# Running sums of a Strassen-like last layer: one three-bank tile against three one-bank tiles

## Chip, cores and metric

The kernel runs on one core of one Trainium2 chip. The metric is the device time of the whole program in microseconds (us). Beside it the profile gives the span: from the first to the last instruction of one profiled execution.

## What is computed

The reference is cut to what matters. All matrices are fp32 in and out.

```python
def _attn_ref(q, k, v, p):                       # q, k, v: 4 x 8 x 576 x 64; p: 4 x 8 x 32 x 64
    p_packed = sm_attn(p, k, v)
    return sm_attn(q, p_packed, p_packed)

def _moe_ref(x, domain_probs, w1, w2):           # x: 2304 x 512, four experts
    p = domain_probs / (domain_probs.sum(-1, keepdims=True) + 1e-09)
    for e in range(E):
        out += p[:, e:e + 1] * (np.maximum(x @ w1[e], 0.0) @ w2[e])

def _moe2_ref(x, w_in, w_out, s, b):             # 512 -> 2048 -> 512
    r = np.maximum(x @ w_in, 0.0)
    g = s * (r * r) + b
    return g @ w_out
```

The change lies in the last function: in `g @ w_out`, and in the order of the steps that make `g`.

## The kernel before

**Stages.** Attention and the four experts fill the first part of the program; the last layer begins to run beside them and has TensorE for itself from about 700 us on. An fp32 product is made of three fp32r matmuls: high part by low part, high by high, low by high.

**The last layer.** The 2048 hidden columns are cut into 4 groups `g` of 512, the 2304 tokens into 3 pairs `tp` of 384-token tiles. One (g, tp) is called a round here; there are 12. In a round both products go by Strassen's scheme (in Winograd's form): seven block products `k`, named "11", "12", "s2", "s1", "s3", "s4", "22" in place of eight. `m3` (matmuls on L1052, 384 columns) is the first product, `x @ w_in`: 7 products times 2 column blocks `j`, which makes 14 units of six matmuls each. Its sums leave PSUM by ACT and DVE (L1109, L1111, L1117, L1118) into `z`.

**The gate.** `z` becomes `g` in place: `q_relu` (L1127, ACT), `q_gate` with n = 0 a square (L1132, ACT) and n = 1 scale and bias (L1134, ACT), for each of four quarters "11", "12", "21", "22" (`f"{c + 1}{j + 1}"`). `q_sum` (L1146, DVE) forms the four Strassen sums of the quarters. `q_part` splits each of the seven operands into the high part (n = 0, L1155, ACT) and the low part (n = 1, L1158, DVE); these are the tiles `gg`.

**The second product.** In the rounds with g = 0 it is `m4` (L1168): plain, 512 columns, 12 matmuls to each of six 128-token blocks; a finished block is copied to `o_sb` by ACT (L1176). In the rounds with g > 0 it is `m4_next` (L1184): for each product `op` in the order `LAST` = "12", "11", "s2", "s1", "s3", "s4", "22" and each 128-token block i = 0, 1, 2 six matmuls of 256 columns. A product adds to a running sum in PSUM: "12", "s1" and "s4" to the right half of a bank (`cols`, h = 1), "11", "s2", "s3" and "22" to the left half (h = 0), bank i for block i. After each product the half is added to `o_sb` by DVE (L1196): all three blocks with one 128x768 instruction, and in the very last round one block at a time, 128x256. The three banks are one tile, `o_ps`. Finished rows go to `out` by SP's queue (L1200).

**The order of the work.** All engines run their own queue in program order, and the program is written by hand. A unit i of the last loop first issues what the table `weave` holds for this step (`at(step, fn, ...)`, L1511 to L1526 for the gate), then the six `m3` matmuls, then a share of the waiting list `todo` (9 matmuls of `m4_next`, about 5 of `m4`). The second product of a round goes on the list four units after its round has ended. So in PE's queue units of 6 + 9 matmuls alternate. After the last unit of `m3` only the list is left: the tail.

**PSUM.** Of 8 banks `o_ps` takes three; five more, "b0" to "b4" of `take_b`, hold `m3`'s sums in turn.

Of the kernel before, what the change touches and what calls it, by code (L numbers as in the profile page):

```python
# [8 lines left out]
F32 = mybir.dt.float32  # L9
# [10 lines left out]
def attention_experts_mlp_kernel(  # L20
# [42 lines left out]
    T3 = 384  # L63
    NT3 = NT // T3
    NS = T3 // P
# [626 lines left out]
    HK = KB // 2  # L692
# [251 lines left out]

    def take_b(name):
        tag = free_b.pop(0)
        return tag, ps_o.tile([P, DM], F32, tag=tag, name=name)

    def x_flip(i, n):
        tag, t = take_b(f"xf_{n}")  # L950
# [6 lines left out]
        )  # L957


    xs, gg, o_sb, sx, yy, o_ps = {}, {}, {}, {}, {}, []  # L960
    xs_dram = {
        (tp, k): dram.tile([P, 2, HK, T3], F32, name=f"xs_dram{tp}{k}")
        for tp in range(NT3 // 2) for k in range(len(OPS))
# [197 lines left out]
    NTP = NT3 // 2  # L1161

    def m4(g, tp, i, f, n):
        acc = o_ps[0][:, i % 3, :]
        y = gg[g, tp, f // 2, i // NS][:, :, f % 2, (i % NS) * P : (i % NS + 1) * P]
        wh, wl = wo_t[g * FG + f]
        lhsT, w = ((y[:, 0], wl), (y[:, 0], wh), (y[:, 1], wh))[n]
        nc.tensor.matmul(  # L1168
            acc, lhsT=lhsT, rhs=w,
            start=(f == 0 and n == 0), stop=(f == FG - 1 and n == 2),  # L1170
        )
        if f == FG - 1 and n == 2:
            t, i = 2 * tp + i // NS, i % NS
            if i == 0:
                o_sb[t] = keep.tile([P, NS, DM], F32, tag="x2", bufs=XB, name=f"o_sb{t}")
            nc.scalar.activation(o_sb[t][:, i, :], acc, AF.Copy)  # L1176

    def m4_next(g, tp, k, i, n):
        op = LAST[k]
        h = int(op in ("12", "s1", "s4"))  # L1180
        cols = slice(h * HK * P, (h + 1) * HK * P)
        r, m = divmod(n, 3)
        x, w = ((0, 1), (0, 0), (1, 0))[m]
        nc.tensor.matmul(  # L1184
            o_ps[0][:, i, cols],
            lhsT=gg[g, tp, k][:, x, r, i * P : (i + 1) * P], rhs=wov[g, k][:, w, r, :],
            start=(n == 0 and op in ("11", "12")), stop=(n == 5), skip_group_check=True,
        )
        end = (g, tp) == (NG - 1, NTP - 1)
        if n == 5 and (end or i == NS - 1):  # L1190
            b = slice(i, i + 1) if end else slice(0, NS)
            c, d = {"11": (0, 0), "12": (0, 0), "s2": (0, 1), "s1": (1, 1), "s3": (1, 1),
                    "s4": (0, 1), "22": (1, 0)}[op]
            t = 2 * tp + c
            dst = o_sb[t][:, b, d * HK * P : (d + 1) * HK * P]
            nc.vector.tensor_tensor(out=dst, in0=o_ps[0][:, b, cols], in1=dst, op=ALU.add)  # L1196
            if g == NG - 1 and op in ("s4", "22"):
                for j in range(b.start, b.stop):
                    r0 = t * T3 + j * P
                    nc.sync.dma_start(out=out[r0 : r0 + P], in_=o_sb[t][:, j])  # L1200


    with tc.manual_schedule():
# [136 lines left out]
        def at(step, fn, *args):  # L1340
            weave.setdefault(step, []).append((fn, args))
# [153 lines left out]
        for g in range(1, NG):  # L1495
            u0 = pos((g * NTP - 1) * UP)
            for q in range(g * NQ, (g + 1) * NQ):
                at(u0 - 5, load_wi, q)
            at(u0 - 2, wi_sums, g, 0)
            for k in range(NK):  # L1500
                at(u0 + 2 * k + 1, wop_parts, g, k)
                if k == 1:
                    at(u0 + 3, wi_sums, g, 1)
                for tp in range(NTP):
                    at(pos((g * NTP + tp) * UP + 2 * k) - 9, xs_load, g, tp, k)
            at(u0 + UP + 1, load_wov, g)
            at(u0 + UP + 4, wov_sums, g, 0)
            at(u0 + UP + 9, wov_sums, g, 1)
            for k in range(NK):
                at(u0 + UP + 6 + 2 * k + 6 * (g == 1 and k > 3), wov_parts, g, k)  # L1510
            for tp in range(NTP):  # L1511
                i = pos((g * NTP + tp) * UP)
                for j in range(NQ):
                    for d, n in ((3, 0), (9, 3), (11, 1)):
                        at(i + d + j, q_relu, g, tp, j, n)
                    for c in range(2):
                        for n in range(2):
                            at(i + 12 + c + j + n, q_gate, g, tp, f"{c + 1}{j + 1}", n)
                for n in range(2):
                    at(i + 14 + n, q_part, g, tp, 1, n)  # L1520
                    at(i + 15 + n, q_part, g, tp, 0, n)
                for d, what in ((16, "s1"), (16, "s2"), (18, "s3"), (19, "s4")):
                    at(i + d, q_sum, g, tp, what)
                for k in range(2, NK):
                    for n in range(2):
                        at(i + 13 + 2 * k + n, q_part, g, tp, k, n)  # L1526
# [34 lines left out]
        stack_a.close()  # L1561
        gb = ctx.enter_context(tc.tile_pool(name="gb", bufs=1, reuse_waits="tile"))
        gate_pool.append(gb)
        ps_o = ctx.enter_context(tc.tile_pool(name="ps_o", bufs=1, space=PSUM, reuse_waits="tile"))
        o_ps.append(ps_o.tile([P, NS, DM], F32, name="o_ps"))
        todo = []
        due = 0.0

# [68 lines left out]
```

## Time and profile before

| | |
|---|---|
| device time, median of 3 runs | 1130.6 us (1122.51 to 1138.27) |
| the profiled execution, its own device time | 1124.23 us |
| its span | 1122.4 us |
| mean granted TensorE clock, share of full speed | 0.996 |
| PE busy | 1065.6 us (95%) |
| DVE busy | 683.6 us (61%) |
| ACT busy | 538.0 us (48%) |

PE is TensorE's matmuls, PEld its weight loads, DVE VectorE, ACT ScalarE, POOL GpSimd, SP the engine that issues the DMAs. A matmul's row begins when it starts and ends when its result is written; matmuls overlap in the array, so a busy PE can still be late. In the views a time in square brackets is how long the engine stood idle before the row, and behind the arrow what released it. A granted clock of 1.00 is 2.4 GHz.

### The profile page before, as it was taken

The numbers are of one execution on the slowest core, as the hardware profiler recorded it, in microseconds if no ns is written. First come the engines' busy times: TensorE is split into PE (matmuls) and PEld (weight loads), VectorE is DVE, ScalarE is ACT, GpSimd is POOL, SyncE is SP. The second block draws the span as 40 slices with busy tenths as digits, with TensorE's granted clock in tenths as the row PEclk, the third lists the DMA queues.
The fourth block names the chain that finished last, engine by engine and source line by source line (L and its number), as shares of the span: only waits on it lengthen the run. The fifth ranks groups of instructions, "written<-read, shape, count | busy, mean of one in ns | idle before, by whom it ended". The sixth has DMA issues, their size and how long they took to land.

```text
span 1122.4 us, 18145 instructions
## 1 busy us (share of the span) xinstructions
PE 1065.6 (95%) x6701; PEld 923.5 (82%) x6701; DVE 683.6 (61%) x1293; ACT 538.0 (48%) x1165; POOL 211.2 (19%) x222
## 2 busy tenths in 40 slices
PE   8999999999999999999999999989898999999975
PEld 5878788888888888888888888877798888888964
DVE  7886755564562455653656457874257676776663
ACT  3533334543442433433357567545555665656650
POOL 1521130321000310103212220120221141141000
PEclk9999999999999999999999999999999999999999
DMA  9765025957865556758552333546454545454411
GB/s 263 186 126 95 3 86 190 307 170 197 256 238 136 145 146 207 236 187 217 150 160 90 108 131 132 225 183 229 166 199 146 188 168 205 169 187 165 164 58 56
DMA packets 106899, 187.09 MB, mean 167 GB/s; under 512 B 49449, under 2 KB 63785, under 8 KB 106811
## 3 DMA queue, kind: packets, MB, share of 16 engines
q1 hardware_dynamic: 106539, 185.87, 52.9%
q8 instruction: 53, 0.87, 0.3%
q14 instruction: 35, 0.29, 0.1%
q10 hardware_dynamic: 272, 0.07, 0.0%
HBM read 131.11 MB, written 54.79 MB: 166 GB/s over the span
## 4 chain that ended last, share of the span: by engine, by line
PE 83%; ACT 8%; DVE 5%; DMA 2%; issue 1%; SPq 0%; ACTq 0%; DVEq 0%
PE acc L889 35%; PE h L843 18%; PE h L1052 11%; PE o_ps L1184 10%; PE o_ps L1168 3%; DVE o_sb L1196 2%; PE pp L625 2%; ACT z L1134 2%; ACT z L1132 1%; DVE qs L1146 1%; DMA v<-in_v_dram 1%; ACT gg L1155 1%; DVE gg L1158 1%; PE pw L539 1%; ACT gg L1023 1%
## 5 line engine op out<-in xcount | busy, mean ns | idle before, releaser
L843 PEld LDWEIGHTS h<-a,w1p 128*128 128x128 f32 x1536 | 229.1, 188 | 27.0 <-issue 5.6
L843 PE MATMUL h<-a,w1p 128*128 128x320 f32 (+1 forms) x1536 | 248.3, 297 | 1.0 <-DVE hl L866 1.0
L866 DVE SCALAR_TENSOR_TENSOR hl<-h,hh 128x256 fp32r<-128x256 f32 x256 | 107.6, 420 | 218.3 <-ACT rest L864 111.6
L1052 PE MATMUL h<-xs,wop 128*128 128x384 f32 x1008 | 205.1, 339 | 1.3 <-DVE xt L910 1.3
L864 ACT ACTIVATE hh<-h 128x256 fp32r<-128x256 f32 x256 | 98.6, 385 | 223.3 <-PE h L843 220.1
L889 PE MATMUL acc<-w2l,hh 128*128 128x512 f32 x512 | 201.7, 394 | 0.0
L889 PE MATMUL acc<-w2h,hh 128*128 128x512 f32 x512 | 201.3, 393 | 0.0
L889 PE MATMUL acc<-w2h,hl 128*128 128x512 f32 x512 | 200.4, 391 | 0.0
L1184 PE MATMUL o_ps<-wov,gg 128*128 128x256 f32 x1134 | 163.2, 288 | 32.9 <-DVE o_sb L1196 22.6
L1184 PEld LDWEIGHTS o_ps<-wov,gg 128*128 128x128 f32 x1134 | 147.0, 190 | 53.1 <-DVE o_sb L1196 16.2
L1052 PEld LDWEIGHTS h<-xs,wop 128*128 128x128 f32 x1008 | 174.5, 190 | 6.3 <-DVE xt L910 1.6
L889 PEld LDWEIGHTS acc<-w2h,hl 128*128 128x128 f32 x512 | 96.2, 188 | 21.9
L889 PEld LDWEIGHTS acc<-w2l,hh 128*128 128x128 f32 x512 | 96.4, 188 | 15.0 <-DVE xt L914 0.3
L889 PEld LDWEIGHTS acc<-w2h,hh 128*128 128x128 f32 x512 | 96.3, 188 | 13.2
L1196 DVE TENSOR_TENSOR o_sb<-o_ps,o_sb 128x768 f32<-128x768 f32 (+1 forms) x77 | 62.4, 810 | 48.3 <-PE o_ps L1184 47.9
L1168 PE MATMUL o_ps<-wo,gg 128*128 128x512 f32 x216 | 61.0, 404 | 12.8 <-ACT o_sb L1176 12.8
L1158 DVE TENSOR_TENSOR gg<-z,gg 128x768 fp32r<-128x768 f32 x45 | 45.2, 1004 | 28.4 <-ACT gg L1155 28.2
L1168 PEld LDWEIGHTS o_ps<-wo,gg 128*128 128x128 f32 x216 | 40.0, 190 | 23.2 <-ACT o_sb L1176 18.0
L688 POOL TENSOR_TENSOR w2l<-w2r,w2h 128x512 fp32r<-128x512 f32 x24 | 31.7, 1329 | 107.7 <-ACT w2h L685 107.6
L1127 ACT ACTIVATE z<-z 128x384 f32<-128x384 f32 x54 | 27.8, 519 | 42.0 <-DVE z L1118 41.8
L633 DVE TENSOR_TENSOR w1o<-pp,w1o 128x512 fp32r<-128x512 f32 x48 | 29.8, 683 | 20.8 <-ACT w1o L632 20.8
L941 ACT ACTIVATE x<-xt 32x384 f32<-32x384 f32 x80 | 41.7, 522 | 1.3
(449 smaller groups left out, 1337.2 us busy)
## 6 DMA issues: line engine op xcount, KB each, us to landing
xs<-xs_dram SPq DMA_DIRECT2D x63, 768.0 KB, 4.2
w1p_dram<-w1o SPq DMA_DIRECT2D x48, 512.0 KB, 4.1
w1p<-w1p_dram SPq DMA_DIRECT2D x192, 128.0 KB, 4.2
xs_dram<-xs SPq DMA_DIRECT2D x21, 768.0 KB, 3.3
w1r<-in_moe_w_dram SPq DMA_DIRECT2D x12, 512.0 KB, 4.4
w2r<-in_moe_w_dram SPq DMA_DIRECT2D x24, 256.0 KB, 5.4
out_dram<-o_sb SPq DMA_DIRECT2D x18, 256.0 KB, 2.1
v<-in_v_dram SPq DMA_DIRECT2D x8, 512.0 KB, 9.6
```

The costliest lines, as they stand in the source:

```text
L633: nc.vector.tensor_tensor(out=t[:, 1], in0=ps[x, z], in1=f32(t[:, 0]), op=ALU.subtract)
L688: nc.gpsimd.tensor_tensor(out=lo, in0=raw_t.pop((e, f)), in1=f32(hi), op=ALU.subtract)
L843: nc.tensor.matmul(t[:, : width(bi, hf)], lhsT=w1p_block(e, bi, f, gi, w), rhs=a2[bi][:, x, gi, part(bi, hf)], start=(n == 0), stop=(n == ...
L864: nc.scalar.activation(hi, src, AF.Relu)
L866: nc.vector.scalar_tensor_tensor(out=lo, in0=src, scalar=0.0, in1=f32(hi), op0=ALU.max, op1=ALU.subtract)
L889: nc.tensor.matmul(acc[j], lhsT=x, rhs=w, start=(f == 0 and n == 0), stop=(g == NF - 1 and n == 2),)
L941: nc.scalar.activation(dst[32 * q : 32 * q + 32, a], src[:, q], AF.Copy)
L1052: nc.tensor.matmul(ps, lhsT=w[:, a, col], rhs=x[:, z, m, :], start=(fresh and n == 0), stop=(n == 3 * HK - 1), skip_group_check=chain,)
L1158: nc.vector.tensor_tensor(out=t[:, 1], in0=src, in1=f32(t[:, 0]), op=ALU.subtract)
L1168: nc.tensor.matmul(acc, lhsT=lhsT, rhs=w, start=(f == 0 and n == 0), stop=(f == FG - 1 and n == 2),)
L1184: nc.tensor.matmul(o_ps[0][:, i, cols], lhsT=gg[g, tp, k][:, x, r, i * P : (i + 1) * P], rhs=wov[g, k][:, w, r, :], start=(n == 0 and op i ...
L1196: nc.vector.tensor_tensor(out=dst, in0=o_ps[0][:, b, cols], in1=dst, op=ALU.add)
```

## The change

Four things change. First, `o_ps` becomes three tiles of one bank each, "o0", "o1", "o2"; in `m4` block i takes tile i % 3, allocated anew for each block. Second, `m4_next` deals the pairs of product and block over the banks in another way: block 1 lies in bank 1 (left or right half as before), blocks 0 and 2 lie side by side in bank 0 for "11", "s2", "s3", "22" and in bank 2 for "12", "s1", "s4". DVE adds block 1 with one 128x256 instruction when it is done, and blocks 0 and 2 with one 128x512 instruction when block 2 is done, in all rounds, the last one included. Third, the pools are split so that "b0" to "b2" take the first three banks, the running sums the next three, "b3" and "b4" the last two. Fourth, in the gate's order the quarters "11" and "12" come one step earlier, and the high and low parts of "12" and "11" come at steps 13 and 14 where they came at 15 and 16 ("12") and at 14 and 15 ("11").

```diff
     def take_b(name):
         tag = free_b.pop(0)
-        return tag, ps_o.tile([P, DM], F32, tag=tag, name=name)
+        pool = ps_x if tag in ("b0", "b1", "b2") else ps_z
+        return tag, pool.tile([P, DM], F32, tag=tag, name=name)
...
     def m4(g, tp, i, f, n):
-        acc = o_ps[0][:, i % 3, :]
+        if f == 0 and n == 0:
+            o_ps[i % 3] = ps_o.tile([P, DM], F32, tag=f"o{i % 3}", name=f"o_{g}{tp}{i}")
+        acc = o_ps[i % 3]
...
     def m4_next(g, tp, k, i, n):
         op = LAST[k]
-        h = int(op in ("12", "s1", "s4"))
-        cols = slice(h * HK * P, (h + 1) * HK * P)
+        b = int(op in ("12", "s1", "s4"))
+        bank = 1 if i == 1 else 2 * b
+        half = b if i == 1 else i // 2
+        if (bank, "next") not in o_ps:
+            o_ps[bank, "next"] = ps_o.tile([P, DM], F32, tag=f"o{bank}", name=f"on_{bank}")
+        ps = o_ps[bank, "next"].rearrange("a (h c) -> a h c", h=2)
...
         nc.tensor.matmul(
-            o_ps[0][:, i, cols],
+            ps[:, half],
             lhsT=gg[g, tp, k][:, x, r, i * P : (i + 1) * P], rhs=wov[g, k][:, w, r, :],
-            start=(n == 0 and op in ("11", "12")), stop=(n == 5), skip_group_check=True,
-        )
-        end = (g, tp) == (NG - 1, NTP - 1)
-        if n == 5 and (end or i == NS - 1):
-            b = slice(i, i + 1) if end else slice(0, NS)
...
-            dst = o_sb[t][:, b, d * HK * P : (d + 1) * HK * P]
-            nc.vector.tensor_tensor(out=dst, in0=o_ps[0][:, b, cols], in1=dst, op=ALU.add)
...
+            start=(n == 0 and i < 2 and (op in ("11", "12") or (op, i) == ("s1", 0))),
+            stop=(n == 5), skip_group_check=True,
+        )
+        if n < 5 or i == 0:
+            return
...
+        src, rows = (ps[:, half], slice(1, 2)) if i == 1 else (ps, slice(0, 3, 2))
+        dst = o_sb[t][:, rows, d * HK * P : (d + 1) * HK * P]
+        if i == 1:
+            dst = dst[:, 0]
+        nc.vector.tensor_tensor(out=dst, in0=src, in1=dst, op=ALU.add)
+        if g == NG - 1 and op in ("s4", "22"):
+            for j in (1,) if i == 1 else (0, 2):
...
-                            at(i + 12 + c + j + n, q_gate, g, tp, f"{c + 1}{j + 1}", n)
+                            at(i + 11 + 2 * c + j + n, q_gate, g, tp, f"{c + 1}{j + 1}", n)
                 for n in range(2):
-                    at(i + 14 + n, q_part, g, tp, 1, n)
-                    at(i + 15 + n, q_part, g, tp, 0, n)
+                    for k in range(2):
+                        at(i + 13 + n, q_part, g, tp, k, n)
...
-        ps_o = ctx.enter_context(tc.tile_pool(name="ps_o", bufs=1, space=PSUM, reuse_waits="tile"))
-        o_ps.append(ps_o.tile([P, NS, DM], F32, name="o_ps"))
+        ps_x, ps_o, ps_z = (
+            ctx.enter_context(
+                tc.tile_pool(name=f"ps_{n}", bufs=1, space=PSUM, reuse_waits="tile")
+            ) for n in "xoz"
+        )
```

PE's queue in the tail before, the first product "12" and the start of "11" of the last round. A row is one matmul or, with x5, five alike; in brackets stand the engines that it waits for.

```order
L1184 MATMUL o_ps<-wov_10626,gg_11419 128x256 [waits DVE_49,Activation_49]
L1184 MATMUL o_ps<-wov_10626,gg_11419 128x256 x5
L1184 MATMUL o_ps<-wov_10626,gg_11419 128x256 [waits DVE_49]
L1184 MATMUL o_ps<-wov_10626,gg_11419 128x256 x5
L1184 MATMUL o_ps<-wov_10626,gg_11419 128x256 [waits DVE_49]
L1184 MATMUL o_ps<-wov_10626,gg_11419 128x256 x5
L1184 MATMUL o_ps<-wov_10671,gg_11407 128x256 [waits DVE_49]
L1184 MATMUL o_ps<-wov_10671,gg_11407 128x256 x5
```

The same place now, with "12" in the tiles on_8981 (bank 2) and on_8988 (bank 1), then "11" in on_9028 (bank 0) and on_8988, then "s2".

```order
L1191 MATMUL on_8981<-wov_10688,gg_11467 128x256 [waits DVE_49,Activation_49]
L1191 MATMUL on_8981<-wov_10688,gg_11467 128x256 x5
L1191 MATMUL on_8988<-wov_10688,gg_11467 128x256 [waits DVE_49]
L1191 MATMUL on_8988<-wov_10688,gg_11467 128x256 x5
L1191 MATMUL on_8981<-wov_10688,gg_11467 128x256 x6
L1191 MATMUL on_9028<-wov_10734,gg_11469 128x256 [waits DVE_49,Activation_49]
L1191 MATMUL on_9028<-wov_10734,gg_11469 128x256 x5
L1191 MATMUL on_8988<-wov_10734,gg_11469 128x256 [waits DVE_49]
L1191 MATMUL on_8988<-wov_10734,gg_11469 128x256 x5
L1191 MATMUL on_9028<-wov_10734,gg_11469 128x256 x6
L1191 MATMUL on_9028<-wov_10779,gg_11530 128x256 [waits DVE_49,Activation_49]
```

Before, each block of six begins with a wait for DVE; now the third block of a product has none, and of two neighbouring products only "11" and "s2" begin in the same bank.

DVE's queue at the same place before, from the last products of the round before (L1196) over the parts of "11" and "12" (L1158) and the Strassen sums (L1146) to the adds of "12":

```order
L1196 TENSOR_TENSOR o_sb_8615<-o_ps,o_sb_8615 128x3x256
L1158 TENSOR_TENSOR gg_11407<-z_11115,gg_11407 128x768
L1196 TENSOR_TENSOR o_sb_8478<-o_ps,o_sb_8478 128x3x256
L1158 TENSOR_TENSOR gg_11419<-z_11139,gg_11419 128x768
L1146 TENSOR_TENSOR qs_32_11436<-z_11115,z_11139 128x768
L1146 TENSOR_TENSOR qs_32_11438<-qs_32_11436,z_11115 128x768
L1196 TENSOR_TENSOR o_sb_8615<-o_ps,o_sb_8615 128x3x256
L1146 TENSOR_TENSOR z_11115<-z_11115 128x768
L1158 TENSOR_TENSOR gg_11449<-qs_32_11438,gg_11449 128x768
L1196 TENSOR_TENSOR o_sb_8745<-o_ps,o_sb_8745 128x256
```

And now:

```order
L1206 TENSOR_TENSOR o_sb_8630<-on_9028,o_sb_8630 128x2x256
L1159 TENSOR_TENSOR gg_11467<-z_11213,gg_11467 128x768
L1159 TENSOR_TENSOR gg_11469<-z_11192,gg_11469 128x768
L1206 TENSOR_TENSOR o_sb_8490<-on_8988,o_sb_8490 128x256
L1206 TENSOR_TENSOR o_sb_8490<-on_8981,o_sb_8490 128x2x256
L1147 TENSOR_TENSOR qs_32_11517<-z_11192,z_11213 128x768
L1147 TENSOR_TENSOR qs_32_11519<-qs_32_11517,z_11192 128x768
L1206 TENSOR_TENSOR o_sb_8630<-on_8988,o_sb_8630 128x256
L1206 TENSOR_TENSOR o_sb_8630<-on_9028,o_sb_8630 128x2x256
L1147 TENSOR_TENSOR z_11192<-z_11192 128x768
L1159 TENSOR_TENSOR gg_11530<-qs_32_11519,gg_11530 128x768
```

The two low parts stand together ahead of the adds of "s4" (o_sb_8490), where before one of them stood behind; every add is two instructions; the two Strassen sums still stand ahead of the adds of "22" (o_sb_8630).

## Rows read from the trace of the kernel before

**Rows 1.** The page, part 1: engine, busy us (share), instructions.

```profile
PE 1065.6 (95%) x6701; PEld 923.5 (82%) x6701; DVE 683.6 (61%) x1293; ACT 538.0 (48%) x1165; POOL 211.2 (19%) x222
```

**Rows 2.** Stretches: window, length; busy PE, PEld, DVE, ACT, POOL; clock, DMA, GB/s.

```profile
702.00:748.00 46.00, 40.23 (x193) 35.16 (x192) 40.05 (x52) 26.67 (x43) 10.37 (x9) 0.96 0.49 194
748.00:817.00 69.00, 61.98 (x299) 53.04 (x298) 27.31 (x46) 34.45 (x60) 10.27 (x8) 1.00 0.58 198
817.00:1079.00 262.00, 243.90 (x1623) 227.85 (x1621) 177.72 (x228) 158.60 (x269) 52.24 (x41) 0.99 0.49 170
1079.00:1123.00 44.00, 25.05 (x162) 20.57 (x162) 20.81 (x35) 8.37 (x11) 0.00 (x0) 0.98 0.19 72
```

**Rows 3.** PE's waits from 690 us: line, releaser, us, times, longest.

```profile
PE o_ps L1184 <- DVE o_sb L1196: 22.6, 29, 2.2
...
PE h L1052 <- DVE xt L910: 1.3, 1, 1.3
```

**Rows 4.** PE's waits in 702 to 748 us, and in 748 to 817 us.

```profile
PE o_ps L1168 <- ACT o_sb L1176: 5.8, 4, 2.0
...
PE o_ps L1168 <- ACT o_sb L1176: 7.0, 8, 1.2
```

**Rows 5.** Timeline at 818 us: start, us, engine, line, instruction, [idle].

```profile
818.44 1.24 PE L1184 MATMUL o_ps<-wov,gg 128*128 128x256 f32 x9
819.52 1.21 PE L1052 MATMUL h<-xs,wop 128*128 128x384 f32 x6
820.57 1.24 PE L1184 MATMUL o_ps<-wov,gg 128*128 128x256 f32 x9
821.64 1.22 PE L1052 MATMUL h<-xs,wop 128*128 128x384 f32 x6
821.91 0.96 DVE L1196 TENSOR_TENSOR o_sb<-o_ps,o_sb 128x768 f32<-128x768 f32 x1 [2.50 <-PE o_ps L1184]
...
823.02 1.30 PE L1184 MATMUL o_ps<-wov,gg 128*128 128x256 f32 x9 [0.16 <-DVE o_sb L1196]
```

**Rows 6.** Timeline around 884 to 890 us: the change of round.

```profile
883.63 2.05 DVE L1146 TENSOR_TENSOR qs<-z,z 128x768 f32<-128x768 f32 x1
...
885.72 1.94 DVE L1146 TENSOR_TENSOR qs<-qs,z 128x768 f32<-128x768 f32 x1
...
888.51 0.94 DVE L1196 TENSOR_TENSOR o_sb<-o_ps,o_sb 128x768 f32<-128x768 f32 x1
...
889.60 1.31 PE L1184 MATMUL o_ps<-wov,gg 128*128 128x256 f32 x9 [2.15 <-DVE o_sb L1196]
```

**Rows 7.** Timeline at 738 us: a wait and the matmuls after it.

```profile
738.80 0.69 PE L1168 MATMUL o_ps<-wo,gg 128*128 128x512 f32 x1 [2.04 <-ACT o_sb L1176]
...
739.28 2.12 PE L1052 MATMUL h<-xs,wop 128*128 128x384 f32 x6
```

**Rows 8.** Timeline of the tail.

```profile
1079.68 2.38 PE L1184 MATMUL o_ps<-wov,gg 128*128 128x256 f32 x18 [1.14 <-DVE o_sb L1196]
...
1081.51 1.02 ACT L1134 ACTIVATE z<-z,b_sb,s_sb 128x768 f32<-128x768 f32 x1
...
1084.25 0.95 DVE L1146 TENSOR_TENSOR qs<-z,z 128x768 f32<-128x768 f32 x1
...
1089.19 0.97 PE L1184 MATMUL o_ps<-wov,gg 128*128 128x256 f32 x6 [1.02 <-DVE o_sb L1196]
...
1090.68 0.98 PE L1184 MATMUL o_ps<-wov,gg 128*128 128x256 f32 x6 [0.52 <-DVE o_sb L1196]
...
1101.04 0.95 DVE L1158 TENSOR_TENSOR gg<-z,gg 128x768 fp32r<-128x768 f32 x1
...
1118.87 0.42 DVE L1196 TENSOR_TENSOR o_sb<-o_ps,o_sb 128x256 f32<-128x256 f32 x1 [1.07 <-PE o_ps L1184]
```

**Rows 9.** DVE's adds by shape: count, busy us, mean ns, idle before.

```profile
L1196 DVE TENSOR_TENSOR o_sb<-o_ps,o_sb 128x768 f32<-128x768 f32 x56 | 53.5, 955 | 31.0 <-PE o_ps L1184 30.5
...
L1196 DVE TENSOR_TENSOR o_sb<-o_ps,o_sb 128x256 f32<-128x256 f32 x21 | 8.9, 424 | 17.3 <-PE o_ps L1184 17.3
```

More of the change, by code (lines that the diff above doesn't have):

```diff
@@ L957, in x_flip @@
         )
-    xs, gg, o_sb, sx, yy, o_ps = {}, {}, {}, {}, {}, []
+    xs, gg, o_sb, sx, yy, o_ps = {}, {}, {}, {}, {}, {}
     xs_dram = {
@@ L1184, in m4_next @@
         nc.tensor.matmul(
-            o_ps[0][:, i, cols],
+            ps[:, half],
             lhsT=gg[g, tp, k][:, x, r, i * P : (i + 1) * P], rhs=wov[g, k][:, w, r, :],
-            start=(n == 0 and op in ("11", "12")), stop=(n == 5), skip_group_check=True,
-        )
-        end = (g, tp) == (NG - 1, NTP - 1)
-        if n == 5 and (end or i == NS - 1):
-            b = slice(i, i + 1) if end else slice(0, NS)
-            c, d = {"11": (0, 0), "12": (0, 0), "s2": (0, 1), "s1": (1, 1), "s3": (1, 1),
-                    "s4": (0, 1), "22": (1, 0)}[op]
-            t = 2 * tp + c
-            dst = o_sb[t][:, b, d * HK * P : (d + 1) * HK * P]
-            nc.vector.tensor_tensor(out=dst, in0=o_ps[0][:, b, cols], in1=dst, op=ALU.add)
[L1197 to L1200, printed above, removed]
+            start=(n == 0 and i < 2 and (op in ("11", "12") or (op, i) == ("s1", 0))),
+            stop=(n == 5), skip_group_check=True,
+        )
+        if n < 5 or i == 0:
+            return
+        c, d = {"11": (0, 0), "12": (0, 0), "s2": (0, 1), "s1": (1, 1), "s3": (1, 1),
+                "s4": (0, 1), "22": (1, 0)}[op]
+        t = 2 * tp + c
+        src, rows = (ps[:, half], slice(1, 2)) if i == 1 else (ps, slice(0, 3, 2))
[5 more added lines that the diff above has]
+            for j in (1,) if i == 1 else (0, 2):
+                r0 = t * T3 + j * P
+                nc.sync.dma_start(out=out[r0 : r0 + P], in_=o_sb[t][:, j])
     with tc.manual_schedule():
```

## The prediction

> **What bounds the kernel now.** I read the page first. PE is busy for 1065.6 of 1122.4 us [rows 1]: TensorE is the bound, and what can be won are its pauses. The list of PE's waits says where they lie. From 690 us on PE waits 22.6 us for DVE's adds (L1196) [rows 3] and 5.8 + 7.0 = 12.8 us for ACT's copies (L1176) [rows 4]; both release the tile `o_ps`. Ahead of 690 us the change touches nothing. The stretches cut this last layer into four: the first round, the other two rounds with `m4`, the rounds in which `m4_next` alternates with `m3`, and the tail [rows 2].
>
> The timeline shows what a wait costs beside its idle time. Without a wait nine matmuls of L1184 go from 818.44 to 819.52, six of L1052 on to 820.57 [rows 5]: 2.13 us for a unit (818.44 to 820.57). At the next product PE starts at 823.02 instead of 821.64 + 1.05 = 822.69, because DVE's 128x768 add, begun at 821.91, takes 0.96 us and six matmuls cover only 1.05 us. Of these 0.33 us only 0.16 us is entered as idle [rows 5]. So the stretch is better judged by its pitch. It holds 1623 matmuls [rows 2], at 15 to a unit 108.2 units; 108.2 x 2.13 = 230.5 us, and it takes 262. 31.5 us are lost, though PE's busy row leaves only 262 - 243.9 = 18.1 us idle [rows 2].
>
> The Trainium skill says the same (page "Trainium Kernel Development and Optimization", section Performance Expectations): matmul busy time is a poor measure of distance to the limit, because matmuls are pipelined. By the busy row this stretch could give back at most 18.1 us, by the pitch 31.5 us; the trace agrees with the page, as the 0.33 us against 0.16 us show.
>
> **What goes: the wait on a whole tile.** In the tail the blocks of one product lie in three different banks, and still the matmuls of a block wait for the add of the block before it: one starts at 1089.19, the next only at 1090.68, after 0.52 us idle that L1196 ended [rows 8]. The wait is thus for the tile, not for the bank. With three tiles, and with products that change between bank 0 and bank 2, a product waits for the add of two products ago. The queue shows two exceptions: "s2" follows "11" in bank 0, and block 1 always lies in bank 1, where the add was made some 12 matmuls earlier.
>
> *Between 817 and 1079 us.* The loss of 31.5 us belongs to about 54 products (1623 / 15 / 2). At the usual 0.25 to 0.33 us each that is 14 to 18 us; the rest, 14 to 18 us, is eight changes of round at some 2 us. There DVE works on the two Strassen sums from 883.63 to 887.66, the add of "22" starts only at 888.51, and PE, ready 2.15 us earlier, starts at 889.60 [rows 6]. With the change "12" begins in bank 2 at once and can run its first six matmuls (0.72 us at 1.08 / 9 each); its block 1 then waits for the small add of "22" in bank 1, which still stands behind the sums. I leave 1 us per change of round (8 us) and 0.25 us for each of eight "s2" (2 us): 31.5 - 10 = 21.5 us, rounded to 22. Bounds: 12 (all eight changes of round stay, and some adds come late) and 30 (nearly all goes).
>
> *`m4`, 702 to 817 us.* ACT's copies cost 5.8 us in four waits of the first round and 7.0 us in eight later ones [rows 4]. A copy is now needed three blocks later. The first round will not return it all: DVE is busy 40.05 of 46 us there [rows 2], so PE can run at most some 6 us faster before DVE bounds it, and its in-order queue is never that tight; I take half, 3 us, and 6 of the 7.0, where DVE is busy 27.31 of 69 us: 9 us, bounds 3 and 13.
>
> The clock: after the longest wait, 2.04 us, six matmuls of L1052 take 2.12 us [rows 7] in place of 1.21 [rows 5], and the granted clock of the stretch is 0.96 [rows 2], between the levels 1.2 and 2.4 GHz. Without the wait that goes: 1 us (0 to 2).
>
> *The pools.* The first `m3` sum after the early units waits 1.3 us for DVE [rows 3]; with "b0" in another bank I take 1 us (-1 to 1.3; another bank may be as late).
>
> *The tail.* Before, 21 blocks of six go at 1.49 us (1089.19 to 1090.68), and the last add ends at 1118.87 + 0.42 = 1119.29 [rows 8]. Now nine products are left when `m3` ends at about 1078.5 (1079.68 - 1.14): "s4", "22" and the seven of the last round. At 18 x 0.119 = 2.14 us each PE needs 19.3 us. DVE runs beside it: nine times a 128x256 add (0.42) and a 128x512 add, whose cost I interpolate from 0.424 and 0.955 us [rows 9] as 0.69; seven low parts at 0.95 and four Strassen sums at 0.95 [rows 8]: 9 x 1.11 + 11 x 0.95 = 20.4 us. The two are nearly equal, so neither hides fully. Followed through the queue: ACT's last gate step ended at 1082.5 and ends there again (the same ACT work in another order), the first Strassen sum starts then instead of at 1084.25 [rows 8], the adds of "22" and "12" come behind two sums each, which holds "12", "11" and "s2" by 1 to 2 us each, and from "s2" on a product takes 2.14 us. That sets PE's end at about 1101.5 and the last add at 1102.3: 17 us less. Two blocks of `out` instead of one leave after it. No row shows what the second costs; it lies between 0 and the 3.1 us that pass now from the last add to the span's end (1122.4 - 1119.29), and I take 1 us: 16 us. Bounds: 10 (each product pays another 0.9 us) and 20 (only PE's 19.3 us and the last add are left).
>
> **What it adds.** DVE makes 63 x 2 = 126 adds for 77. 63 x 1.11 - 62.4 = 7.5 us more; it is busy 177.72 of 262 us, then about 184 of 240. PE's pauses hide it. The gate's steps are moved, not multiplied: on ACT the parts of "12" and "11" pass ahead of three gate steps of the other quarters, which delays the last by at most two such steps of about 1 us (1.02 in [rows 8]), but four gate steps begin a step earlier; the two low parts pass ahead of the adds of "s4" on DVE. If that cover were gone, each round would lose about 1 us, and this lies in the 8 us left above. SP's and POOL's queues keep their order.
>
> **Sum.** 22 + 9 + 1 + 1 + 16 = 49 us. 1124.23 - 49 = 1075. The profiled execution is 6.4 us below the median of the three runs; I add half of this: 1078 us.
>
> **Rivals.**
> *The waits move to the gate.* PE catches up with ACT and DVE and waits for `gg` and for bank 1. For it: DVE's 87% in the first round [rows 2] and its late add at the change of round [rows 6]. Against it: DVE is idle for 84 us between 817 and 1079 us. All terms at their lower bounds: 12 + 3 + 0 - 1 + 10 = 24, 1100 us.
> *The clock falls.* All waits become short pauses within a product, and TensorE is granted 1.2 GHz part of the time. If that held for a quarter of the 230 us, these would take 2.12 / 1.21 = 1.75 times as long: 43 us more, 1121 us. Against it: with a pause at each product the stretch holds 0.99 [rows 2]. The Trainium skill warns of it ("TensorE: Matmul & The Clock Gate", section "A second HAM failure mode: psum-queue depth-cycling"): cycling over PSUM banks makes short idle times that lower the clock again and again. The trace does not bear it out so far.
> *Slower.* Each product now holds bank 1 by an add that DVE issues in the middle of its unit; if that add stands behind a low part that waits for ACT, PE waits in every product. It decides from 49 / 63 = 0.8 us per product on for no gain, and from 1.1 us on for a time above 1147 us (1124 + 23). DVE's idle time allows it, 50 us over 54 products, but its waits would all have to lie there.
> *It does not do what it says*: the waits for DVE stay because the low part of `gg` is awaited at the same matmul. In the queue before, one wait stands for both. Then 1124 us. Against it: where block follows block in the tail, the releaser of each wait is the add [rows 8], and a product has only one low part for its three blocks.
>
> **How the numbers follow.** Forecast 0.74 (1062 to 1092 by itself), waits at the gate 0.16, clock 0.03, slower 0.02, no effect 0.03, rest 0.02. Range 1060 to 1102: down to the upper bounds of the tail and the alternating rounds, up past the first rival. A measurement tells about 2% (23 us) from no change: faster 0.93, same 0.05, slower 0.02.
>
> **What would show it.** Right: the list of PE's waits after keeps under 10 us on the second product's lines in all; products in the alternating rounds start 4.26 us apart; the tail's blocks follow without 0.5 us pauses and the last add ends some 23 us after `m3`. Wrong: waits of PE for DVE or ACT at the gate's parts in the same sum as before, a tail of 35 us or more, a granted clock under 0.95 between 817 and 1079 us, or DVE busy over 90% of that stretch.

## The result, and the profile after

The changed kernel takes 1069.44 us (median of four runs, 1069.13 to 1069.85); the kernel before took 1126.55 us beside it (median of four). The ratio is 0.948, 95% interval 0.940 to 0.956. Over all comparisons the runs of before, and those of e2 below, lie in two groups, 1118.0 to 1125.0 and 1130.6 to 1138.5 us, so their medians move with how many of each there are. The profiled execution took 1069.46 us with a span of 1067.7 us; before it was 1124.23 and 1122.4 us. The forecast was 1078 us, between 1060 and 1102.

The page's first part, which answers to [rows 1]: PE has lost 18.7 busy us and 54.7 us of span.

```profile
PE 1046.9 (98%) x6701; PEld 924.0 (87%) x6701; DVE 687.2 (64%) x1342; ACT 542.2 (51%) x1165; POOL 211.2 (20%) x222
```

The stretches, against [rows 2] (window, length; busy PE, PEld, DVE, ACT, POOL; clock, DMA, GB/s): first round, the other two rounds with `m4`, alternating rounds, tail.

```profile
703.70:746.00 42.30, 42.30 (x212) 37.81 (x211) 40.81 (x58) 24.91 (x42) 10.04 (x8) 1.00 0.61 225
746.00:798.10 52.10, 52.10 (x260) 46.66 (x259) 24.64 (x37) 32.98 (x57) 10.39 (x8) 1.00 0.68 242
798.10:1038.10 240.00, 231.79 (x1606) 226.91 (x1606) 179.34 (x279) 159.46 (x267) 50.48 (x41) 1.00 0.54 184
1038.10:1067.70 29.60, 21.53 (x172) 20.55 (x171) 20.05 (x31) 9.50 (x12) 0.00 (x0) 0.96 0.29 107
```

In the two `m4` windows PE is busy in every microsecond. The granted clock is 1.00 in both and in the alternating rounds.

PE's waits, against [rows 3, 4] (line, releaser, us, times, longest): first from 690 us to the end, then in the alternating rounds. ACT's copies and the 1.3 us of L910 are gone.

```profile
PE on L1191 <- DVE o_sb L1206: 11.1, 14, 1.7
...
PE on L1191 <- DVE o_sb L1206: 7.6, 11, 1.7
```

The list of before has 7.7 us more on the second product's line than [rows 3] shows, put down to ACT:

```profile
PE o_ps L1184 <- ACT uv L1109: 4.0, 2, 2.0
PE o_ps L1184 <- ACT wov L831: 2.4, 2, 1.2
...
PE o_ps L1184 <- ACT gg L1155: 1.3, 1, 1.3
```

These five waits are of the same kind as the others. Each stands at the first matmul of "12", which reads nothing that ACT writes just then, and each time an add of DVE ends 0.14 to 0.15 us before PE starts, as at the waits that are put down to DVE. So before PE waits 30.3 us for the adds, and after 11.1 us.

The timeline at the start of the alternating rounds (start, us, engine, line, instruction), against [rows 5]: from one L1191 row to the next but one it is 4.26 us, 2.13 us for each unit, with no pause where a product ends.

```profile
800.23 1.24 PE L1191 MATMUL on<-wov,gg 128*128 128x256 f32 x9
801.31 1.22 PE L1053 MATMUL h<-xs,wop 128*128 128x384 f32 x6
802.36 1.24 PE L1191 MATMUL on<-wov,gg 128*128 128x256 f32 x9
803.44 1.21 PE L1053 MATMUL h<-xs,wop 128*128 128x384 f32 x6
804.49 0.76 PE L1191 MATMUL on<-wov,gg 128*128 128x256 f32 x5
```

The tail, against [rows 8]: after the last `m3` (1038.11 is the first row without it) three stalls stand behind the sums and their adds, then 90 matmuls follow each other without a break. The last add ends at 1063.83.

```profile
1038.11 6.46 PE L1191 MATMUL on<-wov,gg 128*128 128x256 f32 x51
...
1043.68 0.96 DVE L1147 TENSOR_TENSOR qs<-z,z 128x768 f32<-128x768 f32 x1 [0.94 <-ACT z L1135]
...
1046.02 2.38 PE L1191 MATMUL on<-wov,gg 128*128 128x256 f32 x18 [1.44 <-DVE o_sb L1206]
...
1049.55 1.70 PE L1191 MATMUL on<-wov,gg 128*128 128x256 f32 x12 [1.15 <-DVE o_sb L1206]
...
1052.12 10.97 PE L1191 MATMUL on<-wov,gg 128*128 128x256 f32 x90 [0.87 <-DVE o_sb L1206]
...
1063.14 0.69 DVE L1206 TENSOR_TENSOR o_sb<-on,o_sb 128x512 f32<-128x512 f32 x1 [0.28 <-PE on L1191]
```

This table is read from the timelines of all profiled executions and carries the comparisons below. Times are us; `m4` runs from its first matmul to the first of `m4_next`, "alternating" from there to the first row after the last `m3`, the tail to the end of the span.

| kernel | first `m4` at | `m4` | alternating | tail | span | median of its runs |
|---|---|---|---|---|---|---|
| before | 706.6 | 111.9 | 258.9 | 45.1 | 1122.4 | 1126.6 |
| after | 703.7 | 94.4 | 240.0 | 29.6 | 1067.7 | 1069.4 |
| e1 after, old gate order | 704.9 | 94.9 | 245.9 | 31.4 | 1077.0 | 1079.2 |
| e2 before, new gate order | 706.7 | 115.4 | 254.0 | 44.7 | 1120.8 | 1132.5 |
| e3 three tiles, old dealing | 704.3 | 94.3 | 235.2 | 27.8 | 1061.6 | 1063.3 |
| e4 new dealing, one tile | 705.0 | 116.5 | 295.5 | 43.5 | 1160.5 | 1160.7 |
| e5 after, pools o, x, z | 704.7 | 94.3 | 239.9 | 29.5 | 1068.5 | 1071.2 |
| e6 after, sums later | 703.9 | 94.3 | 249.3 | 31.9 | 1079.4 | 1081.7 |
| e7 e3, sums later | 703.4 | 94.4 | 238.9 | 28.6 | 1065.2 | 1067.4 |
| e8 before, three tiles only | 704.7 | 94.4 | 245.2 | 30.0 | 1074.3 | 1077.3 |
| e9 e3, last weight part later | 707.1 | 94.3 | 233.1 | 27.7 | 1062.3 | 1062.7 |
| e10 e3, all weight parts later | 706.0 | 94.4 | 228.6 | 27.8 | 1056.8 | 1057.5 |
| e11 e1, GpSimd moved | 703.0 | 94.8 | 244.7 | 31.3 | 1073.8 | 1076.2 |
| e12 e10, one part of `wov` later | 702.5 | 94.3 | 228.2 | 27.8 | 1052.8 | 1056.2 |

The gain of 54.7 us of span is 17.5 in `m4`, 18.9 in the alternating rounds, 15.5 in the tail and 2.9 ahead of `m4`. The start differs by up to 5 us between kernels whose work is the same there (702.5 to 707.1), so small differences are read from the later columns. The experiments ran on three chips; a difference of 2 or 3 us between medians alone is not taken as shown.

### The profile page after: what moved, and what is told of

It reads as the page before. It is cut to its first block, busy times and chain, and to the rows that moved or that the text cites. A ratio compares the mean times of both kernels' runs of the same rounds, so it can differ in the third digit from the quotient of the medians.

```text
span 1067.7 us, 18211 instructions
## 1 busy us (share of the span) xinstructions
PE 1046.9 (98%) x6701; PEld 924.0 (87%) x6701; DVE 687.2 (64%) x1342; ACT 542.2 (51%) x1165; POOL 211.2 (20%) x222
## 4 chain that ended last, share of the span: by engine, by line
PE 80%; ACT 8%; DVE 7%; issue 2%; DMA 2%; SPq 1%; ACTq 0%; DVEq 0%
PE acc L889 35%; PE h L843 19%; PE h L1053 10%; PE on L1191 6%; PE o L1171 5%; ACT z L1133 2%; ACT z L1135 2%; PE pp L625 2%; DVE o_sb L1206 1%; DVE gg L1159 1%; ACT gg L1156 1%; DMA v<-in_v_dram 1%; DVE z L1119 1%; ACT z L1128 1%; DVE wop L790 1%
## 5 line engine op out<-in xcount | busy, mean ns | idle before, releaser
L1053 PE MATMUL h<-xs,wop 128*128 128x384 f32 x1008 | 203.0, 337 | 0.0
L1053 PEld LDWEIGHTS h<-xs,wop 128*128 128x128 f32 x1008 | 173.0, 188 | 5.0
L1191 PE MATMUL on<-wov,gg 128*128 128x256 f32 x1134 | 157.2, 283 | 11.7 <-DVE o_sb L1206 11.1
L1191 PEld LDWEIGHTS on<-wov,gg 128*128 128x128 f32 x1134 | 148.6, 189 | 17.4 <-DVE o_sb L1206 15.2
L1206 DVE TENSOR_TENSOR o_sb<-on,o_sb 128x256 f32<-128x256 f32 x126 | 67.3, 552 | 23.4 <-PE on L1191 22.6
L1171 PE MATMUL o<-wo,gg 128*128 128x512 f32 x216 | 57.2, 395 | 0.0
L1171 PEld LDWEIGHTS o<-wo,gg 128*128 128x128 f32 x216 | 39.9, 188 | 5.9 <-DVE gg L1028 0.2
```

The source lines that it names most:

```text
L1053: nc.tensor.matmul(ps, lhsT=w[:, a, col], rhs=x[:, z, m, :], start=(fresh and n == 0), stop=(n == 3 * HK - 1), skip_group_check=chain,)
L1171: nc.tensor.matmul(acc, lhsT=lhsT, rhs=w, start=(f == 0 and n == 0), stop=(f == FG - 1 and n == 2),)
L1191: nc.tensor.matmul(ps[:, half], lhsT=gg[g, tp, k][:, x, r, i * P : (i + 1) * P], rhs=wov[g, k][:, w, r, :], start=(n == 0 and i < 2 and (o ...
L1206: nc.vector.tensor_tensor(out=dst, in0=src, in1=dst, op=ALU.add)
```

## Experiments

My theory was that the separate tiles bring the gain. The rivals were that the dealing over the banks or the gate's new order does. They are taken apart first.

**e8, the three tiles alone**: before, with three tiles of one bank, block i still in bank i, each added alone; old gate order and the running sums in the first three banks as before.

```diff
-        o_ps.append(ps_o.tile([P, NS, DM], F32, name="o_ps"))
+            o_ps[bank, "next"] = ps_o.tile([P, DM], F32, tag=f"o{bank}", name=f"on_{bank}")
...
-            nc.vector.tensor_tensor(out=dst, in0=o_ps[0][:, b, cols], in1=dst, op=ALU.add)
+        nc.vector.tensor_tensor(out=dst, in0=ps[:, half], in1=dst, op=ALU.add)
```

> The kernel before with nothing changed but the tile: three one-bank tiles, block i in bank i, an add to each block, the gate's order and the order of the pools as before. If the gate's order is worth about 10 us as soon as the wait on the tile is gone, whatever the dealing: 1071 to 1076 us. Rival, it was worth that only with the new dealing, where block 1 always shares a bank with the product before: 1064 to 1068 us.

Measured: 1077.29 us, ratio 0.958 (0.951 to 0.964), 1.3 us above the range expected. The tiles alone bring all of the `m4` gain (94.4), nearly all of the tail's (30.0) and 13.7 of the 18.9 us in the alternating rounds. That it is the tile and not the smaller adds, e4 shows next. PE's waits from 690 us:

```profile
PE on L1190 <- DVE o_sb L1202: 9.9, 12, 1.9
PE on L1190 <- ACT gg L1156: 7.2, 4, 2.4
PE h L1053 <- DVE xt L910: 1.3, 1, 1.3
```

The second line looks like waits for the gate, but the four stand at the first matmul of "12" again, and the high part that ACT makes there is that of "s2" (`gg<-qs`). The add of "22" in the same bank ends 0.15 us before PE starts:

```profile
863.97 0.84 ACT L1156 ACTIVATE gg<-qs 128x768 fp32r<-128x768 f32 x1 [4.57 <-DVE qs L1147]
864.33 0.41 DVE L1202 TENSOR_TENSOR o_sb<-on,o_sb 128x256 f32<-128x256 f32 x1
...
864.89 1.32 PE L1190 MATMUL on<-wov,gg 128*128 128x256 f32 x9 [2.41 <-ACT gg L1156]
```

**e4, the dealing alone**: after, with the three banks in one tile again.

```diff
-            o_ps[bank, "next"] = ps_o.tile([P, DM], F32, tag=f"o{bank}", name=f"on_{bank}")
-        ps = o_ps[bank, "next"].rearrange("a (h c) -> a h c", h=2)
+        ps = o_ps["all"][:, bank].rearrange("a (h c) -> a h c", h=2)
```

> The new dealing, the new adds and the new gate's order, but the three banks are one tile again, in the second product of all rounds. Tile theory: no gain, and a loss, since block 2 now also waits for the add of block 1: about 0.5 us for each of 54 products more, less what the last round saves by two adds in place of three, 1130 to 1155 us. Rival, the dealing over banks is what helps: 1070 to 1090 us.

Measured: 1160.69 us, ratio 1.031 (1.024 to 1.038). That is a little slower than I had expected of the tile theory, which it bears out. PE's waits from 690 us:

```profile
PE o_ps L1187 <- DVE o_sb L1202: 62.5, 72, 2.9
PE o_ps L1169 <- ACT o_sb L1177: 14.8, 12, 3.4
```

One of them in the timeline:

```profile
835.19 0.41 DVE L1202 TENSOR_TENSOR o_sb<-o_ps,o_sb 128x256 f32<-128x256 f32 x1
...
835.66 0.98 PE L1187 MATMUL o_ps<-wov,gg 128*128 128x256 f32 x6 [0.63 <-DVE o_sb L1202]
```

Block 2 of a product, six matmuls, waits here for the add of block 1 that lies in another bank. Two adds to a product in one tile make two waits where there was one. The dealing is worth something only with separate tiles, if at all.

**e3, the tiles without the dealing**: after, with block i in bank i and three adds of 128x256.

```diff
-        bank = 1 if i == 1 else 2 * b
-        half = b if i == 1 else i // 2
+        bank, half = i, b
...
-        src, rows = (ps[:, half], slice(1, 2)) if i == 1 else (ps, slice(0, 3, 2))
+        dst = o_sb[t][:, i, d * HK * P : (d + 1) * HK * P]
```

> Three one-bank tiles, but block i stays in bank i and the product's half in the left or right half as before; one 128x256 add to each block, 189 adds. Tile theory: a block waits for the add of the same block one product ago, 12 matmuls earlier, so nothing is lost: 1066 to 1076 us, DVE 63 x (3 x 0.42 - 1.11) = 9 us busier. Rival, a bank must rest (the pairs have to change banks): the first block of each product still waits, 1085 us or more.

Measured: 1063.3 us (1061.97 to 1063.62), ratio 0.944 (0.938 to 0.950): 2.7 us below the range expected and 6.1 us faster than the change itself. In the table 4.8 of it lie in the alternating rounds and 1.8 in the tail, less 0.6 at the start. So the dealing is not needed, and it costs. Of the 4.8 only 1.6 are entered as idle (7.6 against 6.0 us of waits). After has the same stalls at block 1, which lies in bank 1 in every product in both kernels, and more of them; why it has more was not settled. Against e8, e3 has the new gate's order (and the new order of the pools): with the old dealing these two are worth 14 us, 10.0 of them in the alternating rounds, and the four stalls of 7.2 us are gone.

**e2, the gate's order alone**: before with the new order of the gate.

```diff
-                            at(i + 12 + c + j + n, q_gate, g, tp, f"{c + 1}{j + 1}", n)
+                            at(i + 11 + 2 * c + j + n, q_gate, g, tp, f"{c + 1}{j + 1}", n)
...
-                    at(i + 14 + n, q_part, g, tp, 1, n)
-                    at(i + 15 + n, q_part, g, tp, 0, n)
+                    for k in range(2):
+                        at(i + 13 + n, q_part, g, tp, k, n)
```

> The kernel before with the gate's new order and nothing else. Tile theory: the add of "22" still stands behind the two Strassen sums and PE still waits for it, so 1119 to 1126 us by the profile, at most 5 us under the kernel before. Rival, the gate's order is a cause of its own: 1105 to 1115 us.

Measured: ten runs of 1118.0 to 1136.5 us, the profiled one 1122.61, ratio 0.997 (0.991 to 1.004): no change. In the profiled execution it takes 4.9 us off the alternating rounds and adds 3.5 in `m4`, where PE waits 14.8 in place of 12.8 us for ACT's copies.

**e1, the gate's order undone**: after, with the two pieces of that diff taken back.

> The changed kernel with the gate's order of before (parts of "12" and "11" at steps 14 to 16). If the gain comes from the waits on the tile alone, the gate's order is worth 0 to 5 us: 1069 to 1075 us, with PE's waits for DVE in the alternating rounds up by as much. Rival, the gate's order carries a good part of what was won at the changes of round (8 rounds by some 2 us): 1080 us or more.

Measured: 1079.15 us, 9.7 us slower than after (runs of 1078.8 to 1079.8 against 1069.1 to 1069.9). I had expected less; the rival came closer. The order that is worth nothing with one tile is worth nearly 10 us with three: 5.9 in the alternating rounds, 1.8 in the tail, the rest ahead of them, most of it in the start. A change of round in e1:

```profile
861.53 2.03 POOL L818 TENSOR_TENSOR tv<-wv,wv 128x512 f32<-128x512 f32 x1 [25.64 <-DMA wv<-wo_dram]
862.32 2.06 DVE L1147 TENSOR_TENSOR qs<-z,z 128x768 f32<-128x768 f32 x1
...
863.64 1.89 POOL L819 TENSOR_TENSOR wv<-wv 128x512 f32<-128x512 f32 x1
864.41 1.94 DVE L1147 TENSOR_TENSOR qs<-qs,z 128x768 f32<-128x768 f32 x1
...
867.20 1.01 DVE L1206 TENSOR_TENSOR o_sb<-on,o_sb 128x256 f32<-128x256 f32 x2
...
867.67 0.62 PE L1191 MATMUL on<-wov,gg 128*128 128x256 f32 x3 [2.10 <-DVE o_sb L1206]
```

And the same change of round in after, where the two sums take 0.95 us each and GpSimd (POOL) starts only 0.3 us before the second ends; PE does not wait here:

```profile
858.38 0.95 DVE L1147 TENSOR_TENSOR qs<-z,z 128x768 f32<-128x768 f32 x1
859.36 0.96 DVE L1147 TENSOR_TENSOR qs<-qs,z 128x768 f32<-128x768 f32 x1
...
860.02 1.45 POOL L818 TENSOR_TENSOR tv<-wv,wv 128x512 f32<-128x512 f32 x1 [27.16 <-DMA wv<-wo_dram]
```

A sum takes 0.95 us alone and about 2 us when a subtraction of GpSimd is ahead of it. Four of e1's stalls, 2.10, 2.05, 0.91 and 0.86 us, follow such slow sums. The other two at "12", 2.02 and 2.03 us, do not: there both sums take 0.95 us, but behind the low part of "12", which the new order has put out of their way.

```profile
827.84 0.95 DVE L1159 TENSOR_TENSOR gg<-z,gg 128x768 fp32r<-128x768 f32 x1
828.70 0.95 DVE L1147 TENSOR_TENSOR qs<-z,z 128x768 f32<-128x768 f32 x1
829.69 0.96 DVE L1147 TENSOR_TENSOR qs<-qs,z 128x768 f32<-128x768 f32 x1
...
833.89 0.62 PE L1191 MATMUL on<-wov,gg 128*128 128x256 f32 x3 [2.02 <-DVE o_sb L1206]
```

In after the same two stalls are 1.17 and 1.16 us, again with sums of 0.95 us. So 1.7 us of the gain is the order without GpSimd; the four changes of round with slow sums hold 5.9 us of stalls at "12" in e1 and 0.5 in after. Against this, after has two stalls of 1.72 and 1.69 us that e1 has not; they come up again below.

**e11, GpSimd moved**: e1 with the transfer that GpSimd waits for two steps later, and one part of `wov` a step later.

```diff
-            at(u0 + UP + 1, load_wov, g)
+            at(u0 + UP + 3, load_wov, g)
...
-                at(u0 + UP + 6 + 2 * k + 6 * (g == 1 and k > 3), wov_parts, g, k)
+                at(u0 + UP + 6 + 2 * k + 6 * (g == 1 and k > 3) + (k == 5), wov_parts, g, k)
```

> The kernel after with the gate's old order (1079.15 us), and with GpSimd's work moved so that it no longer runs beside the Strassen sums at the change of round: the load of the next `wov` blocks two steps later (GpSimd's two subtractions wait for it), the sixth weight part one step later. Theory: the sums take 2 us in place of 0.95 wherever GpSimd subtracts beside them, and four PE stalls (2.10, 2.05, 0.91, 0.86 us, 5.9 together) come from that, not from the gate's order: the sums take 0.95 us everywhere, the stalls go, 1072 to 1075 us with a tail as before (31 us). Rival: the stalls come from the gate's order itself, the sums standing behind the low part of 12, and are merely longer with slow sums: 1077 to 1080 us.

Measured: 1076.17 us (1075.6 to 1077.6), between the two; of the 3 us only 1.2 lie in the alternating rounds, the rest in the start. The timeline says why:

```profile
859.57 0.95 DVE L1147 TENSOR_TENSOR qs<-z,z 128x768 f32<-128x768 f32 x1
...
860.56 0.96 DVE L1147 TENSOR_TENSOR qs<-qs,z 128x768 f32<-128x768 f32 x1
...
865.47 1.89 POOL L819 TENSOR_TENSOR wv<-wv 128x512 f32<-128x512 f32 x1
866.13 2.04 DVE L1147 TENSOR_TENSOR z<-z,qs 128x768 f32<-128x768 f32 x1
...
868.57 0.62 PE L1191 MATMUL on<-wov,gg 128*128 128x256 f32 x3 [1.22 <-DVE o_sb L1206]
```

The two sums take 0.95 us and the stall of 2.10 us behind them is gone (PE idles 0.02 us there); GpSimd meets the next sum instead, which takes 2.04 us, and a stall of 1.22 us follows that one. The second edit did not part what it was to part: ACT and GpSimd's part moved, and the second sum of the later round still took 1.94 us (stalls 0.91 and 0.86 as before). So the slow sums make the two long stalls of the four (that of 2.05 us goes likewise, and 1.25 us come behind the next sum), as far as this run reaches. How much of the gate's 5.9 us is GpSimd and how much the order, beyond the 1.7 us above, stays open.

**e6 and e7, the sums later**: the Strassen sums behind the adds of "22", in after and in e3.

```diff
-                for d, what in ((16, "s1"), (16, "s2"), (18, "s3"), (19, "s4")):
+                for d, what in ((18, "s1"), (18, "s2"), (20, "s3"), (21, "s4")):
```

> The changed kernel with the Strassen sums of the gate two steps later, behind the adds of "22" in DVE's queue. If what is left at the changes of round is block 1 of "12" waiting for an add behind the sums, most of the 7.6 us of waits between 798 and 1038 us and some 2 us of the tail go: 1059 to 1065 us. Rival, the sums are then late themselves and PE waits for the operand "s2": 1068 us or more, with new waits for DVE or ACT at the gate's parts.

> Three tiles with the old dealing (block i in bank i, three 128x256 adds to a product) and the Strassen sums two steps later. If both effects add: 1063 less the 6.0 us of waits left there and 1 to 2 us of the tail, 1054 to 1059 us. Rival, the sums come too late: 1062 us or more.

Measured: 1081.68 and 1067.35 us, 12.2 and 4.1 us slower than their bases. The wait I meant to remove came back two products on, in e6 for instance at the first block of "s2" as

```profile
876.67 1.34 PE L1191 MATMUL on<-wov,gg 128*128 128x256 f32 x9 [3.01 <-DVE o_sb L1206]
```

**e5, the order of the pools**: after with the pools opened as o, x, z.

> The changed kernel with the running sums in the first three banks, as before, and "b0" to "b4" behind them. If the order of the pools is worth what the step from the experts to the last layer won (1.9 us), 1071 to 1072 us, and the 1.3 us wait of the first sum is back. Rival, the order of the pools is worth nothing: 1069.0 to 1070.0 us.

Measured: 1071.17 us (1069.36 to 1072.1), 1.7 above after with overlapping runs. The old wait of L1053 for L910, 1.3 us, is back; that it costs time is not shown: the first `m4` comes 1.0 us later, within the spread of the start.

**e9, e10 and e12, what is left.** In e3 the longest stalls look like this: DVE stands before a low part of the next weights for 3.70 us, until ACT has made the high part; the add stands behind it.

```profile
853.07 0.76 DVE L790 TENSOR_TENSOR wop<-wi,wop 128x256 fp32r<-128x256 f32 x2 [3.70 <-ACT wop L789]
...
853.75 0.75 DVE L1202 TENSOR_TENSOR o_sb<-on,o_sb 128x256 f32<-128x256 f32 x2
...
854.22 0.62 PE L1190 MATMUL on<-wov,gg 128*128 128x256 f32 x3 [1.70 <-DVE o_sb L1202]
```

e9 moves the last of these parts three steps back, e10 all of them (shown here) and the second sums that GpSimd makes of `w_in`'s next blocks (`wi_sums`); e12 is e10 with `(k == 5)` from e11's diff.

```diff
-                at(u0 + 2 * k + 1, wop_parts, g, k)
+                at(u0 + 2 * k + 2 + 2 * (k == 6), wop_parts, g, k)
...
-                    at(u0 + 3, wi_sums, g, 1)
+                    at(u0 + 4, wi_sums, g, 1)
```

> The kernel with three tiles and the old dealing (1063.4 us profiled), with the sums of the last product's weight parts put three steps later in the first round of a group. Theory: its two longest PE waits, 1.70 and 1.67 us, come from an add that stands on VectorE behind a low weight part which itself waits 3.70 us for ScalarE; with the part moved behind that add they go: 1059.5 to 1061.5 us. Rival: the part is then late for the last product, or only moves the wait to the next add: 1062.5 to 1064 us or more.

> The same kernel with all sums of the next weights' parts one step later (the last three steps later) and the second sums of the expert weights two steps earlier. Theory: all six PE waits of the alternating rounds (6.0 us together) come from VectorE standing behind parts that wait for ScalarE, so most go: 1057 to 1061 us. Rival: the parts then fall in the way of other adds or come late for their products: 1063 us or more.

> The kernel with three tiles, the old dealing and the weight parts later (1057.5 us), with the sixth weight part of `wov` one step later, so that GpSimd's subtraction no longer runs beside the second Strassen sum of two rounds (2.05 us there). Theory: two sums a microsecond shorter, but PE loses only 2 us in all of the alternating rounds: 1055.5 to 1057.5 us. Rival: no cover is missing there, and nothing changes: 1057 to 1058 us; a late part would show as waits for ScalarE or GpSimd and 1059 us or more.

The second sums that e10 moves are those of `w_in`, not of the expert weights, and they come one step later, not two steps earlier as its expectation has it. Measured: e9 1062.68 us: the two long stalls are gone and the alternating rounds 2.1 us shorter, but its profiled start was 2.8 us later, and its runs (1060.43 to 1064.13) overlap e3's. e10 takes 1057.51 us (1055.83 to 1059.67), ratio 0.932 (0.925 to 0.939). Its waits from 690 us:

```profile
PE on L1190 <- DVE o_sb L1202: 3.2, 7, 1.4
```

Its alternating rounds (columns as in the stretches of after):

```profile
800.00:1029.00 229.00, 228.12 (x1609) 226.95 (x1608) 183.78 (x333) 160.28 (x268) 54.95 (x41) 1.00 0.55 194
```

PE is busy 228.12 of 229 us, and at the pace of [rows 5] the stretch's 107 units take 227.9 us: less than 1 us is left in it at this pace. What the move of the sums adds to that of the parts was not taken apart. e12 takes 1056.21 us (1054.57 to 1056.76, six runs); its second sum was still slow (2.05 us) and its stretches equal e10's but for the start, so it tells nothing of GpSimd. Every run of e10 (1059.67 at most) is below every run of e3 (1061.97 at least) and of after: it beats both kernels.

## Why the prediction was right, point by point

*The wait is for the tile.* Right, and shown: `m4` takes 94.3 to 94.9 us in all eleven kernels with three tiles and 111.9 to 116.5 in the three with one, and e8 has 48.1 of the 54.7 us of span with the old dealing and the old gate. Only the size of the wait was read too low, 22.6 us in place of 30.3, because five waits carry ACT's name; the sum was not built on it.

*The alternating rounds, 22 us.* Measured 18.9. From boundary to boundary the stretch holds 1605 matmuls in both kernels, 107 units, or 227.9 us at 2.13 each. Before it takes 258.9, a loss of 31.0 us, as reckoned; after it takes 240.0, a loss of 12.1 where I had left 10 and rounded up. The long stalls of before are ten, 14.8 us in all, around six changes of round; I had counted eight. The places of the residue were half right: stalls at block 1 of "12" in the changes of round (1.17, 1.16, 0.33 and 0.21 us), but the longest (1.72 and 1.69 us) come from low weight parts that wait for ACT, which I did not see; e9 and e10 remove the like of them in e3.

*`m4`, 9 us.* Mis-sized: 17.5. The step that failed is "PE can run at most some 6 us faster before DVE bounds it, and its in-order queue is never that tight". DVE is busy 40.81 of 42.30 us and PE waits for nothing. All 12.8 us of waits went, and another 4.7 us that were not entered as idle. One part is the clock: in the 4.00 us behind the longest wait of [rows 7] the granted clock is 0.57, between its levels 1.2 and 2.4 GHz, and in the rest of the stage 1.00, which by estimate costs 4.00 x 0.43 = 1.7 us, where I had put 1.

```profile
738.80:742.80 4.00, 4.00 (x12) 3.63 (x13) 2.99 (x4) 2.28 (x4) 0.00 (x0) 0.57 0.34 137
```

The other 3 us, by difference, are some 0.25 us at each of the twelve waits, of the kind that [rows 5] shows with 0.33 against 0.16 us. I had used the pitch in place of the idle time for the alternating rounds and did not do so here.

*The tail, 16 us.* Measured 15.5. PE's last 90 matmuls run at 0.12 us each as reckoned (18 to a product). The last add ends 25.7 us after `m3`; predicted were 23.8 from 1078.5, or 25.0 from the boundary used here, 1077.3 in before. "12", "11" and "s2" are held by 1.44, 1.15 and 0.87 us, where the prediction had 1 to 2 us each; the second block of `out` costs 0.8 us (1067.7 - 1063.83 = 3.87, against 3.11 before) where I took 1.

*The pools, 1 us.* The wait of 1.3 us is gone, and back in e5; that it was worth 1 us is not shown, since e4, which has the new pools and not the wait, starts `m4` at 705.0 and e5 at 704.7. The 128x512 add, estimated at 0.69 us, takes 0.67 to 0.69.

*The gate's order, costed at nothing.* Here the sum was right only as a whole. I gave the order no term; undone, it costs 9.7 us. The step that failed is "The gate's steps are moved, not multiplied", read as worth nothing: what counts is which instruction stands ahead of the sums and the adds in DVE's queue. And I gave the dealing the credit for the products that wait for "the add of two products ago"; it costs 6 us. The gain that I booked under the tiles at the change of round came from tiles and gate together: with one tile the earlier sums meet another wait (e2), without the tile they decide.

*The rivals.* Waits for `gg` do not appear in after; the sign "under 10 us" of waits was missed by a little (11.1), all of it waits for the adds. The granted clock did not fall: 1.00 in every stretch but the tail. The Trainium skill's warning that cycling over PSUM banks lowers the clock ("TensorE: Matmul & The Clock Gate", section "A second HAM failure mode: psum-queue depth-cycling") is not borne out by this case. The slower outcome, an add behind a low part that waits for ACT, is real but rare: two stalls of 1.7 us, not one in every product.

## What to carry to other kernels

Before changing how work is dealt over memory, see what the wait guards: blocks in separate banks waited for each other because they were one tile, and three tiles with nothing else changed brought 48 of 55 us of span. An edit that measures as nothing alone (the gate's order) can be worth 10 us or more once the wait in front of it is gone, and one that seems part of the remedy (the dealing) can cost; take each away from the finished kernel as well as adding it to the old one. When one wait on an in-order engine is gone, look next at what stands ahead of the awaited instruction in its queue and itself waits: moving those few instructions by a step gave another 6 us.

## What was not expected of the hardware

A sum of DVE from SBUF to SBUF takes 0.95 us alone and up to 2.06 us when a subtraction of GpSimd has started before it; GpSimd's own goes from 1.29 to as much as 2.05 us when DVE is first. DVE's adds that read PSUM are not touched: in the alternating rounds of after the 128x512 add takes 0.67 to 0.69 us in 32 instances without GpSimd beside it and 0.68 to 0.69 us in 21 with. The prediction had read the 2.05 and 1.94 us of [rows 6] as what such a sum takes there, with 0.95 us in [rows 8] before its eyes. GpSimd's row of before at that place, and then a case in after:

```profile
883.58 1.29 POOL L818 TENSOR_TENSOR tv<-wv,wv 128x512 f32<-128x512 f32 x1 [28.41 <-DMA wv<-wo_dram]
...
890.48 1.28 POOL L832 TENSOR_TENSOR wov<-wv,wov 128x512 fp32r<-128x512 f32 x1 [2.54 <-ACT wov L831]
...
890.53 2.05 DVE L1147 TENSOR_TENSOR qs<-qs,z 128x768 f32<-128x768 f32 x1
```

In the last two rows GpSimd starts 0.05 us earlier and keeps its 1.28 us; DVE ends 0.82 us after it, so nearly its whole 0.95 us follows. The Trainium skill states this ("SBUF — State Buffer", section "SBUF: two separate sides"): an operation of DVE with two SBUF inputs and one of GpSimd that reads SBUF exclude each other for the whole instruction. The trace agrees.
